# Retention attention followed by a gated two-layer product: the order of the first four pieces' loads and copies, and who copies the last quarter

## The chip, the cores and the metric

The kernel runs on 1 core of one Trainium2 chip. The metric is the time of one execution on the device in microseconds (us). The engines are named as the profile names them: PE (TensorE: matmuls and transposes; PEld is its weight load), ACT (ScalarE), DVE (VectorE), POOL (GpSimd), SP (SyncE, which here only issues DMAs). ACTq and POOLq are the instruction queues of those engines. Each engine takes its instructions in the order written.

## What is computed

The reference, cut to what matters (8 batches, 8 heads, 576 positions, 64 features a head; 4608 tokens, 512 columns, 2048 hidden columns):

```python
scores = (1 / sqrt(D)) * q @ k.transpose(0, 1, 3, 2)
gamma  = 1 - 2 ** (-5 - arange(H))
rel    = pos[:, None] - pos[None, :]
Dmat   = where(rel >= 0, gamma[:, None, None] ** rel, 0)
x      = ((scores * Dmat) @ v)            # then heads side by side: 4608 x 512
h      = x @ w_in                          # 4608 x 2048
g      = h * clip(h + 3, 0, 6) / 6
out    = g @ w_out                         # 4608 x 512, float32
```

## The kernel before

**Pieces.** The sequence of a batch is cut into pieces of 128 positions (four a batch, 32 "main" pieces), and the last 64 positions of two batches make one "rest" piece. The decay is split into a factor on q (`gq`), a factor on v (`gv`, spread out as `gqv[:, 1]`), a 0/1 mask and a state carried from piece to piece. A piece needs: q and k transposed (`qk`, features on partitions), scores `sc` = k q, the masked scores `at` (DVE), v scaled (`vs`, `scale_v`, DVE, in place), the output `o` = `vs` with `at` plus the carried state `tbd` with q, and the new state `u` = k with `vs` plus the old one, scaled by `gfull` into the next `tbd` (DVE). `o` is copied by ACT into `xt`, the input of the first large product.

**The large products.** They go by blocks `kb` of 512 tokens (nine of them). `g1` multiplies `xt` with `win16` (line L577), ACT and DVE make the gate (L585, L586); `g2` (L635), and from the third block `g2_seven` (L720), multiply with `wout16`. Block 0 is made of pieces 0 to 3, so its `g1` can't start before these four are done; later pieces are worked in between units of the large products, in an order written out by hand.

**The first four pieces (`EARLY` = 4)** are worked before any large product. Their k and v come by POOL's queue, which casts them from float32 to float16 on the way (`load_third`, L103; 128 KB written each), in the order k0 v0 k1 v1 k2 v2 k3 v3, then the five parts of `win16`, then the `wout16` parts and later pieces. Their q come plain in float32 by SP's queue into buffers `qf` (`load_q`, L120; 256 KB each), and ACT casts them (`cast_q`, L128). `load_q` can be given an instruction that must be done before the transfer is issued. q is then transposed and scaled in one step by 8 matmuls with `dq`, the diagonal matrices of `gq` (`q_by_pe`); k by 4 transposes (`k_by_pe`); ACT copies each of the two from PSUM into `qk`. In the last of the four, q is copied in two halves, the mask is done in two halves (`scores_last`) and the output too (`out_last`).

`warm` issues matmuls on zeros into a spare PSUM bank. `later` holds DVE operations (mask, state) that `run_later` issues.

Before, the order in the first stretch is:
- q0 and q1 are sent at once; q2 waits for the matmuls of `q_by_pe(0)`, q3 for the transposes of `k_by_pe(0)`.
- DVE: scaling of v0, mask 0, state 0, then per piece c: scaling of v, mask, state.
- ACT: casts, copies, and the two copies that fill `gfull` (L193, L195).

**The end.** In the last block `g2_seven` ends with product x in two PSUM tiles, one for each half u of the last quarter of the output. `copy_half` (L751) copies each on ACT into a buffer `osb`, and `store` (L625) sends it in two halves of 64 rows, one issued by SP and one by ACT. The quarters before go through `total` (L741, DVE) and `store_quarter` (L688): one half from SP, the other from ACT. The `osb` buffers rotate over four.

Of the kernel before, what the change touches and what calls it, by code (L numbers as in the profile page):

```python
# [13 lines left out]
ALU = mybir.AluOpType  # L14
# [3 lines left out]
def kernel(  # L18
# [16 lines left out]
    nc = tc.nc  # L35
    B, H, S, D = q.shape
    NTOK, DM = out.shape
    DFF = moe_w_in.shape[1]
    P = 128
    NPAIR = H // 2  # L40
# [84 lines left out]
                reason="the first pieces have the queues")  # L125

    def cast_q(c):
        nc.scalar.copy(loaded[c]["q16"], plain_q[c])  # L128

    def load_win(f0, f1):  # L130
        return nc.gpsimd.dma_start(
# [11 lines left out]
    nc.gpsimd.iota(wide, pattern=[[1, P + 1]], base=-1, channel_multiplier=-1,  # L143
                   allow_small_or_imprecise_dtypes=True)
    load_q(0)
    load_q(1)
    load_kv(0)
    zeros = const.tile([P, MBLK], FP16)
    nc.vector.memset(zeros, 0.0)
# [6 lines left out]
    for h in range(H):  # L156
# [15 lines left out]
    nc.vector.tensor_tensor(out=ident16, in0=mask01, in1=mask_wide[:, 0:P], op=ALU.subtract)  # L172

    dq = const.tile([P, H, P], FP16)
    nc.vector.tensor_tensor(out=dq, in0=ident16[:, None, :].to_broadcast([P, H, P]),
                            in1=gq[:, :, None].to_broadcast([P, H, P]), op=ALU.mult)
    gqv = const.tile([P, 2, H, D], FP16)
    cast_q(0)
    nc.scalar.copy(gqv[:, 1], gv[:, :, None].to_broadcast([P, H, D]))
# [10 lines left out]
    nc.vector.memset(gfull, 0.0)  # L190

    def fill_gfull():
        nc.scalar.copy(gfull[0:HALF, :, 0:D],  # L193
                       gc[0:HALF, 0, :, None].to_broadcast([HALF, NPAIR, D]))
        nc.scalar.copy(gfull[HALF:P, :, D:2 * D],  # L195
                       gc[HALF:P, 0, :, None].to_broadcast([HALF, NPAIR, D]))

    def fill_gq():
        nc.scalar.copy(gqv[:, 0], gq[:, :, None].to_broadcast([P, H, D]))
# [52 lines left out]
    def k_by_pe(c, tag=None):  # L252
        kn = loaded[c]["kn"]
        pk = bank_or(tag, [P, NPAIR, P], FP16, name=f"trk_{c}")
        for p in range(NPAIR):
            newest[0] = nc.tensor.transpose(pk[:, p, :], kn[:, 2 * p:2 * p + 2, :], ident16)
        nc.scalar.copy(qk_of(c)[:, 1], pk)

    def q_by_pe(c):
        q16, qk = loaded[c]["q16"], qk_of(c)  # L260
        pq = bank([P, NPAIR, P], FP32, name=f"trq_{c}")
        for p in range(NPAIR):
            for h2 in range(2):
                r = slice(h2 * HALF, h2 * HALF + HALF)
                newest[0] = nc.tensor.matmul(
                    pq[r, p, :], q16[:, 2 * p + h2, :], dq[:, 2 * p + h2, :],
                    start=(p == 0), stop=(p == NPAIR - 1), skip_group_check=True)
        if c == EARLY - 1:
            for p in (0, 2):
                nc.scalar.copy(qk[:, 0, p:p + 2], pq[:, p:p + 2])  # L270
        else:
            nc.scalar.copy(qk[:, 0], pq)

    def scores_last(c):

# [60 lines left out]
    def scores(c, late=9):  # L336
        run_later(late)
        qk = st[c]["qk"]
        sc = psum.tile([P, 2, NPAIR, P], FP32, tag="sc", name=f"sc_{c}")
        for p in range(NPAIR):  # L340
            for h2 in range(2):
                r = slice(h2 * HALF, h2 * HALF + HALF)
                nc.tensor.matmul(sc[:, h2, p, :], qk[r, 1, p, :], qk[r, 0, p, :],
                                 start=True, stop=True)
        at = work.tile([P, 2, NPAIR, P], FP16, tag="at", bufs=3, name=f"at_{c}")
        st[c]["at"] = at
        later.append(lambda: nc.vector.tensor_tensor(
            out=at.rearrange("t a b s -> t (a b) s"), in0=sc.rearrange("t a b s -> t (a b) s"),
            in1=mask_b, op=ALU.mult))
# [328 lines left out]
    def store_quarter(kb, i, j, src):  # L678

        cols = slice(NH * j, NH * j + NH)  # L680
        if kb < B:
            r0 = kb * S + TH * i
            nc.sync.dma_start(out[r0:r0 + TH, cols].rearrange("(u p) n -> p u n", u=2), src)
        else:
            rest = out.rearrange("(m x s) n -> x s m n", x=2, s=S)
            for x in range(2):
                queue = nc.scalar if x else nc.sync
                queue.dma_start(rest[x, MAIN:S, 2 * i:2 * i + 2, cols],  # L688
                                src[x * HALF:x * HALF + HALF])

    def g2_seven(kb, last=False):

        gt = gts[kb]

        def w(i, j):
            return wout16[:, KH * i:KH * i + KH, NH * j:NH * j + NH]

        def a(i, j):
            return gt[:, KH * j:KH * j + KH, TH * i:TH * i + TH]

        def s(name):
            return sums[kb, name]

        acc = {}

        def get(name):
            if name not in acc:
                if last and name == "x":
                    acc[name] = [psum.tile([P, NH], FP32, tag=t, name=f"x{t}_{kb}")
                                 for t in ("o", "tu")]  # L710
                else:
                    whole = bank([P, 2, NH], FP32, name=f"{name}_{kb}")
                    acc[name] = [whole[:, 0], whole[:, 1]]
                    wholes[name] = whole
            return acc[name]

        def product(name, u, left, right, first):
            dst = get(name)[u]
            for c in range(KH):
                newest[0] = nc.tensor.matmul(  # L720
                    dst, left()[:, c, P * u:P * u + P], right[:, c, :],
                    start=(first and c == 0 and (u == 0 or name not in wholes)),
                    stop=(c == KH - 1), skip_group_check=True)

        kept, wholes = {}, {}

        def parts(name, tile):
            if name in wholes:
                return [(wholes[name], tile)]
            return [(acc[name][u], tile[:, u]) for u in range(2)]  # L730

        def keep(name):
            kept[name] = work.tile([P, 2, NH], FP32, tag="keep_" + {"m5": "m1"}.get(name, name), bufs=1,
                                   name=f"keep_{name}_{kb}")
            for src, dst in parts({"m5": "z"}.get(name, "x"), kept[name]):
                nc.scalar.copy(dst, src)

        def total(i, j, name, src):
            osb = work.tile([P, 2, NH], FP32, tag="osb", bufs=4, name=f"osb_{kb}_{i}_{j}")
            for (a0, dst), (_, a1) in zip(parts(src, osb), parts(src, kept[name])):  # L740
                nc.vector.tensor_tensor(out=dst, in0=a0, in1=a1, op=ALU.add)  # L741
            store_quarter(kb, i, j, osb)

        def copy_total():
            osb = work.tile([P, 2, NH], FP32, tag="osb", bufs=4, name=f"osb_{kb}_1_0")
            nc.scalar.copy(osb, wholes["x"])
            store_quarter(kb, 1, 0, osb)

        def copy_half(u):
            osb = work.tile([P, NH], FP32, tag="osb", bufs=4, name=f"osh_{kb}_{u}")  # L750
            nc.scalar.copy(osb, acc["x"][u])  # L751
            store(kb, 2 + u, slice(0, NH), osb)

        def unit(name, u, left, right, first, then=()):
            def do():
                product(name, u, left, right, first)
                for f in then:
                    f()
            return do

        plan = [
            ("x", lambda: a(0, 0), w(0, 0), True, [lambda: keep("m1")]),
            ("y", lambda: a(0, 1), w(1, 0), True,
             [lambda: total(0, 0, "m1", "y"), lambda: token_sums(kb, "s3")]),
            ("x", lambda: s("s2"), wts["t2"], False, [lambda: keep("u2")]),
            ("z", lambda: s("s1"), wts["t1"], True,
             [lambda: keep("m5"), lambda: token_sums(kb, "s4")]),
            ("x", lambda: s("s3"), wts["t3"], False, [lambda: total(1, 1, "m5", "x")]),
            ("z", lambda: s("s4"), w(1, 1), False, [lambda: total(0, 1, "u2", "z")]),
            ("x", lambda: a(1, 1), wts["t4"], False, [] if last else [copy_total]),  # L770
        ]
        units = []
        for n, (name, left, right, first, then) in enumerate(plan):
            for u in range(2):
                after = then if u else []
                if last and n == len(plan) - 1:
                    after = [lambda u=u: copy_half(u)]
                units.append(unit(name, u, left, right, first, after))
        return units
# [12 lines left out]
            load(4)  # L792
        load_wout(4 * i, 4 * i + 4)

    scale_v(0)
    q_by_pe(0)
    load_q(2, newest[0])
    warm(2, MBLK)
    cast_q(1)
    k_by_pe(0)  # L800
    load_q(3, newest[0])
    fill_gfull()
    for c in range(EARLY):
        if c:
            inter(c - 1)
# [1 line left out]
        if c < EARLY - 1:  # L807
            scores(c)
            run_later(9)
            if c:  # L810
                k_by_pe(c + 1)
            state_early(c)
            run_later(9)
            if not c:
                k_by_pe(c + 1)
            q_by_pe(c + 1)
            if c + 2 < EARLY:
                cast_q(c + 2)
            scale_v(c + 1)
        else:  # L820
            scores_last(c)
# [280 lines left out]
```

## Time and profile before

| | us |
|---|---|
| median of 3 runs | 294.99 |
| lowest and highest | 293.27, 295.82 |
| the profiled execution's own time | 294.43 |
| its span in the profile | 292.6 |
| PE busy | 281.1 (96%) |
| DVE busy | 227.6 (78%) |
| ACT busy | 169.1 (58%) |
| POOL busy | 104.3 (36%) |
| granted clock of PE | 1.0 |

The profile shows one execution. The page lists busy time by engine, the span in 40 slices, the DMA queues, the chain of work that ended last, and groups of instructions. A row of the timeline gives the start in us, the duration, the engine, the line, the operation, what it writes and reads, and in brackets how long the engine had been idle before and what ended that. For a DMA, "to landing" is the time from the start of its issue to the last of its data.

### The profile page before, as it was taken

The page shows a single profiled execution, that of the slowest core. Times are in us where ns is not written, and L with a number is a line of the kernel's source. Part 1 is how long each engine was busy: PE and PEld are TensorE (multiplying, and loading weights), DVE is VectorE, ACT ScalarE, POOL GpSimd, SP SyncE. Part 2 cuts the span into 40 slices and gives each one's busy share as a digit, 9 for nine tenths or more (in the row PEclk, how much of TensorE's full clock was granted, in tenths as well). Part 3 has the DMA queues.
Part 4 walks back from the last instruction along what each step waited for, and adds up shares of the span by engine and source line. Part 5 has one row for each costly group of instructions (what it writes and reads, how often), then busy time and mean ns, then how long its engine had stood idle before and what let it go on. Part 6 is the DMA issues. An engine that isn't in the chain of part 4 may idle for free.

```text
span 292.6 us, 8351 instructions
## 1 busy us (share of the span) xinstructions
PE 281.1 (96%) x3492; PEld 174.7 (60%) x3492; DVE 227.6 (78%) x377; ACT 169.1 (58%) x301; POOL 104.3 (36%) x130
## 2 busy tenths in 40 slices
PE   7699999999989999999999999999999999999993
PEld 2454445544544587458745874587458745874682
DVE  4858656798758997899789988998899588728860
ACT  6668537784357744774486448644864286338711
POOL 8753578159523432443234324455550000000000
PEclk9999999999999999999999999999999999999999
DMA  9999999999999989997999799979992240120014
GB/s 137 177 205 203 191 157 215 165 126 137 132 215 166 160 85 120 168 141 81 121 163 143 77 127 170 136 82 123 160 139 47 74 110 0 38 81 30 0 39 109
DMA packets 156631, 36.21 MB, mean 124 GB/s; under 512 B 143792, under 2 KB 155568, under 8 KB 156592
## 3 DMA queue, kind: packets, MB, share of 16 engines
q0 software_dynamic: 113104, 17.83, 89.3%
q1 hardware_dynamic: 42896, 17.31, 30.5%
q8 instruction: 27, 0.44, 0.7%
q10 hardware_dynamic: 592, 0.52, 0.5%
q14 instruction: 12, 0.10, 0.1%
HBM read 36.70 MB, written 9.44 MB: 158 GB/s over the span
## 4 chain that ended last, share of the span: by engine, by line
PE 91%; DMA 4%; POOL 2%; DVE 1%; issue 1%; ACT 0%; ACTq 0%; POOLq 0%
PE ph L577 41%; PE x L720 14%; PE pout L635 9%; PE z L720 8%; PE y L720 5%; DMA kn<-in_k_dram 3%; PE o L483 3%; PE sc L450 2%; PE o L504 1%; PE u L535 1%; PE ph L600 1%; POOL kn L103 1%; DMA out_dram<-osb 1%; PE xtu L720 1%; PE xo L720 1%
## 5 line engine op out<-in xcount | busy, mean ns | idle before, releaser
L577 PE MATMUL ph<-xt,win 128*128 128x512 f16 x560 | 122.3, 379 | 0.0
L586 DVE SCALAR_TENSOR_TENSOR gt<-u,ph 128x512 f16<-128x512 f32 x144 | 95.7, 685 | 22.6 <-ACT u L585 21.4
L585 ACT ACTIVATE u<-ph,cb 128x512 f32<-128x512 f32 x144 | 98.4, 688 | 25.7 <-PE ph L577 25.1
L577 PEld LDWEIGHTS <-win 128*128 128x128 f16 x560 | 54.7, 98 | 64.4
L103 POOL DMA_DIRECT2D kn<-in_k_dram x40 | 34.0, 850 | 40.7 <-PE ph L577 15.4
L103 POOL DMA_DIRECT2D qv<-in_v_dram x40 | 33.8, 846 | 38.8 <-PE ph L577 16.2
L720 PEld LDWEIGHTS <-sum_s 128*128 128x128 f16 x448 | 42.7, 98 | 5.3
L103 POOL DMA_DIRECT2D qv<-in_q_dram x36 | 30.2, 839 | 28.7 <-PE z L720 10.4
L720 PEld LDWEIGHTS <-gt 128*128 128x128 f16 x336 | 32.1, 98 | 5.5
L635 PE MATMUL pout<-wout,gt 128*128 128x512 f16 x128 | 29.6, 379 | 0.1
L720 PE MATMUL x<-wsum_t,sum_s 128*128 128x256 f16 x192 | 22.9, 273 | 0.0
L556 ACT CAST tm<-th 128x256 f16<-128x256 f32 x24 | 9.7, 405 | 20.3 <-DVE th L551 20.1
L635 PEld LDWEIGHTS <-gt 128*128 128x128 f16 x128 | 11.9, 98 | 13.2 <-issue 0.4
L456 DVE TENSOR_TENSOR at<-sc,mask 128x1024 f16<-128x1024 f32 x14 | 17.0, 1217 | 1.9 <-PE sc L450 1.9
L676 DVE TENSOR_TENSOR sum_s<-gt 128x1024 f16<-128x1024 f16 (+1 forms) x21 | 18.1, 864 | 0.2
L332 DVE TENSOR_TENSOR qv<-qv,gqv 128x1024 f16<-128x1024 f16 x26 | 17.8, 684 | 0.0
L514 ACT CAST xt<-o 128x512 f16<-128x512 f32 x28 | 15.0, 585 | 4.6 <-PE o L504 4.6
L567 DVE TENSOR_TENSOR ta<-u,th 128x256 f32<-128x256 f32 x24 | 10.2, 424 | 6.3 <-ACT th L554 5.2
L720 PE MATMUL z<-wout,sum_s 128*128 128x256 f16 x112 | 14.5, 274 | 0.0
L720 PE MATMUL y<-wout,gt 128*128 128x256 f16 x112 | 14.3, 273 | 0.0
L720 PE MATMUL z<-wsum_t,sum_s 128*128 128x256 f16 x112 | 13.6, 273 | 0.0
L720 PE MATMUL x<-wout,gt 128*128 128x256 f16 x96 | 11.5, 272 | 0.0
(118 smaller groups left out, 255.3 us busy)
## 6 DMA issues: line engine op xcount, KB each, us to landing
out_dram<-osb SPq DMA_DIRECT2D x32, 256.0 KB, 3.2
kn<-in_k_dram POOLq DMA_DIRECT2D x32, 128.0 KB, 5.9
qv<-in_v_dram POOLq DMA_DIRECT2D x32, 128.0 KB, 6.0
qv<-in_q_dram POOLq DMA_DIRECT2D x28, 128.0 KB, 5.9
wout<-in_moe_w_out_dram POOLq DMA_DIRECT2D x4, 512.0 KB, 15.2
win<-in_moe_w_in_dram POOLq DMA_DIRECT2D x3, 512.0 KB, 12.3
qf<-in_q_dram SPq DMA_DIRECT2D x4, 256.0 KB, 4.6
win<-in_moe_w_in_dram POOLq DMA_DIRECT2D x2, 256.0 KB, 8.3
```

The lines of the kernel that those rows point to most:

```text
L103: loaded[c]["dma"].append(nc.gpsimd.dma_start(dst[p0:p0 + n], src[b, :, s0:s0 + n, :].rearrange("h s d -> s h d")))
L332: scaled = nc.vector.tensor_tensor(out=qv, in0=qv, in1=gqv, op=ALU.mult)
L456: nc.vector.tensor_tensor(out=at.rearrange("t a j p s -> t (a j p) s"), in0=sc.rearrange("t a j p s -> t (a j p) s"), in1=mask64[:, None, ...
L514: nc.scalar.copy(xt_at(cs[0], 0, 2 * P).rearrange("e p (j x s) -> e p j x s", j=2, x=2) [:, :, :, half, :], o[half].rearrange("e j p s -> ...
L556: nc.scalar.copy(tm, ta)
L567: nc.vector.tensor_tensor(out=ta, in0=st[c]["u"][1], in1=st[c]["sum"], op=ALU.add)
L577: newest[0] = nc.tensor.matmul(ph, win16[:, dmc, P * fc:P * fc + P], xt_of(kb)[:, dmc, :], start=(dmc == 0), stop=(dmc == NCC - 1))
L585: nc.scalar.activation(u, ph, ACTF.Relu, bias=cb[:, 0:1], scale=1.0 / 6.0)
L586: nc.vector.scalar_tensor_tensor(out=gts[kb][:, fc, :], in0=u, scalar=1.0, in1=ph, op0=ALU.min, op1=ALU.mult)
L635: nc.tensor.matmul(pout, gt[:, fc, P * mc:P * mc + P], wout16[:, fc, :], start=(fc == 0), stop=(fc == NFC - 1))
L676: nc.vector.tensor_tensor(out=s(which)[:, c0:c1], in0=x(), in1=y(), op=op)
L720: newest[0] = nc.tensor.matmul(dst, left()[:, c, P * u:P * u + P], right[:, c, :], start=(first and c == 0 and (u == 0 or name not in whol ...
```

## The change

- `load_q(1)` is no longer sent at once. q1 waits for the DVE instruction that makes `dq`, and q2 and q3 follow it without a wait of their own.
- ACT's casts of q1 to q3 come later in its order: q(c+1) is cast after the scores of piece c are issued.
- DVE does mask 0 ahead of the scaling of v0 (before: after it).
- The two copies that fill `gfull` go from ACT to DVE, ahead of everything of piece 0.
- The order on PE within the loop changes: piece 0's state comes after the transposes of k1 and q1; in the later pieces the state comes ahead of the next piece's transposes, and in the third turn of the loop q3 is transposed ahead of k3.
- In the last of the four pieces k, not q, is copied in two halves.
- One more `warm` matmul stands between k0's transposes and the scores of piece 0.
- At the end, the second half of the last quarter is copied by DVE instead of ACT, and one half of the quarter with j = 1 in the first row of quarters is stored from POOL instead of ACT.
- `newest` is now set in `scores` instead of `q_by_pe`. Its other uses come after a later matmul that sets it again.

```diff
     load_q(0)
-    load_q(1)
     load_kv(0)
...
-    nc.vector.tensor_tensor(out=dq, in0=ident16[:, None, :].to_broadcast([P, H, P]),
-                            in1=gq[:, :, None].to_broadcast([P, H, P]), op=ALU.mult)
+    load_q(1, nc.vector.tensor_tensor(
+        out=dq, in0=ident16[:, None, :].to_broadcast([P, H, P]),
+        in1=gq[:, :, None].to_broadcast([P, H, P]), op=ALU.mult))
+    for c in range(2, EARLY):
+        load_q(c)
...
     def fill_gfull():
-        nc.scalar.copy(gfull[0:HALF, :, 0:D],
-                       gc[0:HALF, 0, :, None].to_broadcast([HALF, NPAIR, D]))
-        nc.scalar.copy(gfull[HALF:P, :, D:2 * D],
-                       gc[HALF:P, 0, :, None].to_broadcast([HALF, NPAIR, D]))
+        nc.vector.tensor_copy(gfull[0:HALF, :, 0:D],
+                              gc[0:HALF, 0, :, None].to_broadcast([HALF, NPAIR, D]))
+        nc.vector.tensor_copy(gfull[HALF:P, :, D:2 * D],
+                              gc[HALF:P, 0, :, None].to_broadcast([HALF, NPAIR, D]))
...
-        nc.scalar.copy(qk_of(c)[:, 1], pk)                      # k_by_pe
+        if c == EARLY - 1:
+            for p in (0, 2):
+                nc.scalar.copy(qk_of(c)[:, 1, p:p + 2], pk[:, p:p + 2])
+        else:
+            nc.scalar.copy(qk_of(c)[:, 1], pk)
...
-        if c == EARLY - 1:                                      # q_by_pe
-            for p in (0, 2):
-                nc.scalar.copy(qk[:, 0, p:p + 2], pq[:, p:p + 2])
-        else:
-            nc.scalar.copy(qk[:, 0], pq)
+        nc.scalar.copy(qk[:, 0], pq)
...
-                queue = nc.scalar if x else nc.sync             # store_quarter, last block
+                queue = (nc.gpsimd if j > i else nc.scalar) if x else nc.sync
...
-            nc.scalar.copy(osb, acc["x"][u])                    # copy_half
+            if u:
+                nc.vector.tensor_copy(osb, acc["x"][u])
+            else:
+                nc.scalar.copy(osb, acc["x"][u])
...
-    scale_v(0)
+    fill_gfull()
     q_by_pe(0)
-    load_q(2, newest[0])
     warm(2, MBLK)
-    cast_q(1)
     k_by_pe(0)
-    load_q(3, newest[0])
-    fill_gfull()
+    warm(1, MBLK)
     for c in range(EARLY):
         if c:
             inter(c - 1)
             intra(c - 1)
         if c < EARLY - 1:
             scores(c)
             run_later(9)
+            cast_q(c + 1)
             if c:
-                k_by_pe(c + 1)
-            state_early(c)
-            run_later(9)
+                state_early(c)
+                run_later(9)
+            else:
+                scale_v(c)
+            if c == EARLY - 2:
+                q_by_pe(c + 1)
+            k_by_pe(c + 1)
+            if c < EARLY - 2:
+                q_by_pe(c + 1)
             if not c:
-                k_by_pe(c + 1)
-            q_by_pe(c + 1)
-            if c + 2 < EARLY:
-                cast_q(c + 2)
+                state_early(c)
+                run_later(9)
             scale_v(c + 1)
```

More of the change, by code (lines that the diff above doesn't have):

```diff
@@ L127, in cast_q @@
     def cast_q(c):
-        nc.scalar.copy(loaded[c]["q16"], plain_q[c])
+        return nc.scalar.copy(loaded[c]["q16"], plain_q[c])
     def load_win(f0, f1):
@@ L264, in q_by_pe @@
                 r = slice(h2 * HALF, h2 * HALF + HALF)
-                newest[0] = nc.tensor.matmul(
-                    pq[r, p, :], q16[:, 2 * p + h2, :], dq[:, 2 * p + h2, :],
-                    start=(p == 0), stop=(p == NPAIR - 1), skip_group_check=True)
-        if c == EARLY - 1:
-            for p in (0, 2):
-                nc.scalar.copy(qk[:, 0, p:p + 2], pq[:, p:p + 2])
-        else:
-            nc.scalar.copy(qk[:, 0], pq)
+                nc.tensor.matmul(pq[r, p, :], q16[:, 2 * p + h2, :], dq[:, 2 * p + h2, :],
+                                 start=(p == 0), stop=(p == NPAIR - 1), skip_group_check=True)
+        nc.scalar.copy(qk[:, 0], pq)
     def scores_last(c):
@@ L342, in scores @@
                 r = slice(h2 * HALF, h2 * HALF + HALF)
-                nc.tensor.matmul(sc[:, h2, p, :], qk[r, 1, p, :], qk[r, 0, p, :],
-                                 start=True, stop=True)
+                newest[0] = nc.tensor.matmul(sc[:, h2, p, :], qk[r, 1, p, :], qk[r, 0, p, :],
+                                             start=True, stop=True)
         at = work.tile([P, 2, NPAIR, P], FP16, tag="at", bufs=3, name=f"at_{c}")
```

## The prediction

> **What bounds the kernel now.** I read the slices of the page first, to see where TensorE (PE) isn't full.
>
> ```profile
> PE   7699999999989999999999999999999999999993
> PEclk9999999999999999999999999999999999999999
> DMA  9999999999999989997999799979992240120014
> ```
>
> Each digit is a slice of 7.3 us. PE is below 9 in the first two or three slices and in the last; the clock is full throughout. Next the table by windows, for how much that is, and PE's waits after the first main matmul.
>
> ```profile
> 0.00:18.17 18.17, 13.11 (x153) 7.14 (x153) 11.87 (x37) 12.05 (x26) 14.60 (x22) 1.00 1.56 166
> ...
> 120.00:287.80 167.80, 167.71 (x2157) 112.32 (x2154) 137.76 (x213) 95.28 (x165) 40.84 (x52) 1.00 0.90 96
> 287.80:292.60 4.80, 0.00 (x0) 0.00 (x0) 0.00 (x0) 0.40 (x2) 0.00 (x0) 1.00 0.42 111
> ```
>
> ```profile
> PE o L504 <- issue: 0.9, 1, 0.9
> PE o L372 <- DVE qv L245: 0.5, 1, 0.5
> PE o L303 <- DVE at L286: 0.3, 1, 0.3
> ```
>
> The columns after the window are its length and busy PE, weight loads, DVE, ACT, POOL. From 18.17 to 287.8 PE waits 1.7 us in all at most (0.9 of it for nothing that the profile shows, and the 0.3 of L303 falls at 17.9). So the time is A, the start of the first main matmul (L577, 18.17), plus B, a fixed 269.6 of full PE, plus C, the tail of 4.8. The change edits what decides A and C; in B it changes nothing but the start. For A, the chain of waits in the first 25 us:
>
> ```profile
> 6.75 7.55 DMA kn<-in_k_dram
> 14.30 0.05 issue
> 14.34 0.40 PE trk L256 x4
> ...
> 16.20 0.37 PE sc L283 x8
> 16.57 0.02 issue
> 16.59 1.30 DVE at L286 x2
> 17.89 0.04 issue
> 17.93 0.30 PE o L303 x4
> 18.23 6.80 PE ph L577 x31
> ```
>
> The last early K (issued 6.75) lands at 14.30, and A follows 3.87 later. For C, the ACT timeline of the end:
>
> ```profile
> 284.71 2.64 ACTq L688 DMA_DIRECT2D out_dram<-osb  x2
> 287.45 0.37 ACT L751 COPY osh<-xo 128x256 f32<-128x256 f32 x1 [4.30 <-DMA out_dram<-osb]
> 287.86 0.51 ACTq L625 DMA_DIRECT2D out_dram<-osh  x1
> 288.49 0.37 ACT L751 COPY osh<-xtu 128x256 f32<-128x256 f32 x1 [0.66 <-ACT osh L751]
> 288.89 0.51 ACTq L625 DMA_DIRECT2D out_dram<-osh  x1
> ```
>
> PE's last two groups (xo, xtu) end at 286.84 and 287.71. The copy of xo starts only at 287.45: the wait is put down to a DMA, but the store that used that buffer belongs to the block before. What stands ahead of it in ACT's queue is the issue of a store (286.7, 0.63 us). Copy, issue, copy, issue then run in series on ACT, and the last store is issued at 288.89, 1.2 after PE is done.
>
> **The tail (C), step by step.** That half store moves to POOL, so ACT is free when xo ends: copy 286.9 to 287.27, issue at 287.3. The second copy goes to DVE, idle since 286.7: from 287.76, 0.42 us (DVE's add of the same 128x256 shape, L741, took 0.42; a copy reads one operand less), so done at 288.18, and SP and ACT issue the last stores at 288.2 instead of 288.89. SP has two issues of 0.5 to 0.6 from 286.7 on and is free at 287.9. The last store then lands 2.0 to 2.2 later as before (L625), and the end follows. Gain: 0.65 us. The POOL store's cost isn't in the trace, POOL having written nothing to memory; nearest are its 64-row loads (L103 after 200 us): issue 0.68, landing 2.8 to 5.3 after the start of the issue, median 3.9, against 2.5 to 2.9 for the ACT store. From 286.7 that is 289.5 to 292.0; the last store lands at 290.3. I take 3.9 (290.6, a cost of about 0.2 against the gain in the worst reading) as hidden, since the 5.3 belongs to the time when loads queued; the bounds are 0 and 1.7. Nothing is queued behind it on POOL.
> The Trainium skill, "DMA: Bandwidth & Descriptors", Latency and other measured facts, speaks against moving a store there: first byte at about 1 us from GpSimd, 0.6 from SP and ACT. By that page the store would land 0.4 later than ACT's 2.9, near 290.0, still covered; no row here shows a POOL store.
>
> **The front (A): when data lands.** Landing is the issue plus the time to landing of single issues. Before: Q0 3.96, Q1 5.26, K0 6.12, V0 7.01, K1 7.91, V1 8.69, Q2 10.49, K2 11.04, V2 12.85, Q3 13.37, K3 14.30, V3 15.08, first weights 16.15. These follow the order in which the issues end, whichever queue they are on (V1 5.05, Q2 5.70, K2 5.93, V2 6.80, Q3 6.96, K3 7.68). So it is one line of transfers, always full, and moving the Qs reorders it without shortening it.
> After: SP's Q1 waits for the dq operation of DVE (2.37 plus 1.23, 3.60). Queued behind it on SP are Q2 and Q3, and then only the output store of 42.11. The three issues end near 4.1, 4.5 and 4.9; POOL's K0, V0, K1, V1 at 2.4, 3.3, 4.2, 5.05. Order: Q0 K0 V0 Q1 K1 Q2 Q3 V1 K2 V2 K3 V3.
> Prices: a K or V 0.88 (V0 to K1 0.90, K1 to V1 0.78). A Q: 0.99 (256 KB at the 265 GB/s of the window 3 to 4 us) to 1.47 (V1 to K2 is 2.35, less 0.88); Q0 to Q1 is 1.30, with the start-up in it. I take 1.2. K0 without Q1 ahead: 1.36 plus the 3.4 to 3.7 of an unhindered load, and 0.15 for its longer issue, 5.2.
> Sums: V0 6.1, Q1 7.3, K1 8.2, Q2 9.4, Q3 10.6, V1 11.4, K2 12.3, V2 13.2, K3 14.1, V3 15.0. K0 is 0.9 sooner, which buys nothing: the two warm matmuls hold PE to 6.1. K3 is 0.2 sooner, but K2 is 1.3 later and V1 2.7 later.
>
> **The front: what follows from it.** Durations are the rows of before (casts and copies on ACT 0.59 to 0.62, the next one 0.49 after; mask 1.23; state scaling 0.69; V scaling 0.42; transposes 0.40).
> Piece 0: transposes 6.1, its scores 7.2, as now; the extra warm matmul (about 0.45) lies in the 0.7 that PE waits for ACT's copy. The two fills, now on DVE, cost 0.40 each on ACT; on DVE they run from 5.4 to about 6.2, where DVE idles to 7.11; cover gone, they would delay the first mask by 0.8. First mask ahead of first scaling saves nothing, since V0 lands before the scores exist.
> Piece 1: K1 8.2, copies of K and Q to 9.7, scores 9.8 (before 9.52). Then DVE has V1's scaling ahead of mask 1, and V1 lands at 11.4: mask 1 runs 11.85 to 13.1 (before 9.95). This is the new wait; behind it on DVE stand the state of piece 1, V2's scaling and mask 2.
> Piece 2: K2 12.3, transposes to 12.75, copies of K and Q to 13.9, scores 13.95, mask 2 14.4 to 15.6.
> Piece 3: PE's queue has scores 2, state 2, Q3, K3. Q3's cast stands behind the output copy of piece 1 on ACT (13.9 and 14.4 to 15.0), so Q3 goes at 15.05 and K3's transposes at 15.3, though K3 has been there since 14.1. Copy of Q3 15.45, K3 in halves from 15.95, scores 16.3 (before 16.13), masks 16.65 to 17.95, outputs, A at 18.4. K in halves shortens K3 to A from 3.87 to 3.1, but K3 no longer decides: K2 plus 6.1 does.
> The first weights land 1.07 after V3, at 16.1; they don't bind. The second quarter landed at 20.43 before and is used at 21.6, so A may move by 0.3 freely.
>
> **The sum.** Front +0.25 (18.4 less 18.17), tail -0.65: -0.4. The profiled execution took 294.43 (span 292.6 and 1.8 around it); it gives 294.0. It lay 0.19% under the median of 294.99, and the runs span 293.27 to 295.82, so the range needs about a microsecond each way for that alone.
>
> **Rivals.** (1) Slower: all three Qs go ahead of K1 on the engines. For it: from 8.0 to 8.5 us, with Q2 in flight, the DMA engines moved almost only Q2's rows (197 GB/s against 143 to 148 with K and V alone). Against: Q3, issued at 6.59, let V2 pass. Then K1 lands at 10.6, its chain (K1 plus 8.6, a mask, a state scaling and a V scaling per piece on DVE) puts A at 19.2: +1.05 - 0.65 = +0.4, 294.8; with a Q at 1.47 K1 is at 11.4, A at 20.0, 295.6. It decides from K1 landing after 10.2. (2) The Qs cost 0.99 and don't hold up K2: K2 11.7, A 17.8, or, if K2 stays at 11.0, K3 13.8 plus 3.3 is 17.1; total -1.0 to -1.7, 292.7 to 293.4. For it: fewer switches between queues; against: the mixed rows above. (3) POOL's store lands last, 5.3 after its issue, at 292.0: the end is 0.9 later than before instead of 0.65 sooner, 295.6. That the Qs are not sent together can't be: behind Q1's wait SP has nothing else to wait for.
> The Trainium skill, "DMA: Bandwidth & Descriptors", Queues, rings and completion order, has each DMA engine take packets from its queues in turn, not by arrival. By that rule V1 goes ahead of Q3 and lands near 10.3, mask 1 runs earlier, and A is 18.3, 0.1 under my sum. The trace's V2 ahead of Q3 speaks for arrival.
>
> **How the numbers follow.** Forecast 0.52 (its own range 293.0 to 295.2), rival 1 0.22, rival 2 0.18, rival 3 0.08. All lie within 1.5 us of before, and 1% (2.95 us) is about what a measurement of this kernel can tell from no change. Faster by over 1% needs the best of rival 2 and a low run, 0.07; slower by over 1% rivals 1 and 3 together or a high run, 0.08; within 1% 0.85. Range: rival 2 less half a microsecond of spread, 292.3, to rivals 1 and 3 with a little, 296.0.
>
> **What would show it.** Right: Qs landing ahead of V1 and K2; DVE's wait before mask 1 or the scaling ahead of it put down to V1; PE no longer waiting for K3; the first main matmul at 17.8 to 18.8; ACT's copy of xo at 286.9 plus the shift of A, DVE's copy beside it, and the last issue 0.5 after PE's end instead of 1.2. Wrong: K1 after 10.2, K2 before 11.5, a POOL store landing after the last ACT store, or a B other than 269.6.

## The result and the profile after

| | before | after |
|---|---|---|
| median (18 runs each, same chip) | 293.86 | 295.98 |
| lowest and highest | 293.05, 295.82 | 294.42, 297.77 |
| the profiled execution (span) | 294.43 (292.6) | 295.67 (293.9) |

The changed kernel is slower: ratio 1.0064, interval 1.0043 to 1.0085. The forecast was 0.4 us faster. After's page starts like this:

```profile
PE   7699999999999999999999999999999999999993
PEclk9799999999999999999999999999999999999999
```

The slices of PE look almost as before; only the second digit of the clock row is lower. The table by windows, cut at the start of the first main matmul (19.70) and near the end of PE's work, shows what moved (columns as in the prediction).

```profile
0.00:19.70 19.70, 15.19 (x154) 8.04 (x154) 12.56 (x39) 11.20 (x24) 14.57 (x22) 0.91 1.46 157
19.70:289.41 269.71, 268.04 (x3343) 167.50 (x3340) 215.72 (x340) 156.52 (x274) 90.10 (x109) 1.00 1.18 121
289.41:293.90 4.49, 0.00 (x0) 0.00 (x0) 0.42 (x1) 0.00 (x0) 0.00 (x0) 0.98 0.43 119
```

In before PE's last matmul ended at 287.71, so its three parts are 18.17, 269.54 and 4.94. After has A +1.53, B +0.17, C -0.45: together +1.25, and the two profiled executions differ by 1.24. The loss is in the front. PE's waits say where it begins:

```profile
PE trk L258 <- DMA kn<-in_k_dram: 2.2, 1, 2.2
...
```

This wait is new: PE stands 2.2 us for K1. In before K1's transposes had no wait on their row:

```profile
7.96 0.40 PE L256 MATMUL trk<-ident,kn 128*128 128x128 f16 x4
```

Before's waits for K2 (1.17) and K3 (1.00) are gone, since PE now comes to them later. The timeline of after's front, PE and DVE:

```profile
7.14 0.40 PE L344 MATMUL sc<-qk 64*128 64x128 f16 x8 [0.25 <-ACT qk L263]
9.71 0.40 PE L258 MATMUL trk<-ident,kn 128*128 128x128 f16 x4 [2.17 <-DMA kn<-in_k_dram]
...
11.48 0.61 PE L344 MATMUL sc<-qk 64*128 64x128 f16 x8
...
13.32 0.61 PE L258 MATMUL trk<-ident,kn 128*128 128x128 f16 x4
...
16.49 0.40 PE L258 MATMUL trk<-ident,kn 128*128 128x128 f16 x4
```

```profile
11.77 0.43 DVE L247 TENSOR_TENSOR qv<-qv,gqv 128x512 f16<-128x512 f16 x1
12.13 1.22 DVE L348 TENSOR_TENSOR at<-sc,mask_wide 128x1024 f16<-128x1024 f32 x1
```

K1's transposes start at 9.71 (9.67 is its landing), V1 is scaled the moment it lands (11.74), mask 1 follows at 12.13, K2's transposes start at 13.32 (landing 13.27). K3's start at 16.49 without a wait in brackets, a microsecond after K3 landed (15.46). From 10.4 to 13.8 PE's groups take 0.59 to 0.64 instead of 0.40, which is the lower clock.

Landings, last of the 16 engines:

| | K0 | V0 | Q1 | K1 | Q2 | V1 | K2 | V2 | Q3 | K3 | V3 |
|---|---|---|---|---|---|---|---|---|---|---|---|
| before | 6.12 | 7.01 | 5.26 | 7.91 | 10.49 | 8.69 | 11.04 | 12.85 | 13.37 | 14.30 | 15.08 |
| forecast | 5.2 | 6.1 | 7.3 | 8.2 | 9.4 | 11.4 | 12.3 | 13.2 | 10.6 | 14.1 | 15.0 |
| after | 4.87 | 7.83 | 9.11 | 9.67 | 10.84 | 11.74 | 13.27 | 14.62 | 14.79 | 15.46 | 16.35 |

From V0 on everything is later than forecast, and the line ends 1.3 later than before. The DMA engines' rate shows where the line falls behind. Window 3 to 4 us of before, then of after; the last column is GB/s:

```profile
3.00:4.00 1.00, 1.00 (x4) 0.18 (x2) 0.82 (x6) 0.01 (x1) 1.00 (x2) 1.00 1.29 265
```

```profile
3.00:4.00 1.00, 1.00 (x4) 0.17 (x2) 0.83 (x6) 0.23 (x1) 1.00 (x2) 1.00 1.47 105
```

Q0's packets end at 3.1 in before and 3.3 in after. In before Q1's follow at once (middle packet, the start of the median one of its 1024, 3.55) and then K0's (4.51), V0's (5.41), K1's (6.32). In after nothing follows but K0 (3.84) and V0 (5.20), whose POOL issues end at 2.40 and 3.29; Q1, issued at 3.6, comes at 6.41 and K1 at 7.38. Through V0 after has moved one Q (256 KB) less and is only 0.2 sooner.

The tail of after:

```profile
288.57 0.37 ACT L755 COPY osh<-xo 128x256 f32<-128x256 f32 x1 [3.73 <-PE xo L721]
288.69 0.62 POOL L689 DMA_DIRECT2D out_dram<-osb  x1 [69.11 <-DVE osb L742]
288.97 1.43 ACTq L626 DMA_DIRECT2D out_dram<-osh  x2
289.10 1.42 SPq L626 DMA_DIRECT2D out_dram<-osh  x2
289.44 0.42 DVE L753 COPY osh<-xtu 128x256 f32<-128x256 f32 x1 [1.06 <-PE xtu L721]
```

ACT's copy now waits for PE's xo and nothing else, DVE copies xtu right after PE's end (289.41), and the last stores are issued at 289.9, 0.5 after it (before: 1.2).

### The profile page after: what moved, and what is told of

Read it like the earlier page. It is cut to its first block, busy times and chain, and to the rows that moved or that the text cites. A ratio compares the mean times of both kernels' runs of the same rounds, so it can differ in the third digit from the quotient of the medians.

```text
span 293.9 us, 8353 instructions
## 1 busy us (share of the span) xinstructions
PE 283.2 (96%) x3493; PEld 175.5 (60%) x3493; DVE 228.7 (78%) x380; ACT 167.7 (57%) x298; POOL 104.7 (36%) x131
## 4 chain that ended last, share of the span: by engine, by line
PE 92%; DMA 3%; DVE 1%; issue 1%; POOL 1%; ACT 1%; POOLq 0%
PE ph L578 41%; PE x L721 14%; PE pout L636 9%; PE z L721 9%; PE y L721 5%; DMA qv<-in_v_dram 3%; PE o L484 3%; PE sc L451 2%; PE o L505 1%; PE u L536 1%; PE ph L601 1%; PE xtu L721 1%; PE xo L721 1%; PE trk L258 1%; POOL kn L103 1%
## 5 line engine op out<-in xcount | busy, mean ns | idle before, releaser
L721 PEld LDWEIGHTS <-sum_s 128*128 128x128 f16 x448 | 42.7, 98 | 5.3
L103 POOL DMA_DIRECT2D qv<-in_q_dram x36 | 30.2, 839 | 30.9 <-PE z L721 10.4
L721 PEld LDWEIGHTS <-gt 128*128 128x128 f16 x336 | 32.1, 98 | 5.5
L689 POOL DMA_DIRECT2D out_dram<-osb x1 | 0.6, 617 | 69.1 <-DVE osb L742 69.1
L721 PE MATMUL x<-wsum_t,sum_s 128*128 128x256 f16 x192 | 22.9, 273 | 0.0
L568 DVE TENSOR_TENSOR ta<-u,th 128x256 f32<-128x256 f32 x24 | 10.2, 424 | 6.8 <-ACT th L555 5.8
L721 PE MATMUL z<-wout,sum_s 128*128 128x256 f16 x112 | 14.5, 274 | 0.0
L721 PE MATMUL y<-wout,gt 128*128 128x256 f16 x112 | 14.3, 273 | 0.0
L721 PE MATMUL z<-wsum_t,sum_s 128*128 128x256 f16 x112 | 13.6, 273 | 0.0
```

What stands on the lines that cost most here:

```text
L103: loaded[c]["dma"].append(nc.gpsimd.dma_start(dst[p0:p0 + n], src[b, :, s0:s0 + n, :].rearrange("h s d -> s h d")))
L568: nc.vector.tensor_tensor(out=ta, in0=st[c]["u"][1], in1=st[c]["sum"], op=ALU.add)
L721: newest[0] = nc.tensor.matmul(dst, left()[:, c, P * u:P * u + P], right[:, c, :], start=(first and c == 0 and (u == 0 or name not in whol ...
```

## The experiments

Two theories of the loss were tried first: that the late Qs make K1 late, and that the front runs at half the clock because PE stands still. "Rate" is the mean over 3 to 4 us, A the start of the first main matmul; ratios are to the kernel before on the same chip. Rate, landings and A are of one profiled execution of each kernel. The low rate of after from 3 to 4 us is called the hole.

| kernel | ratio (95%) | rate | K1 | K2 | V3 | A |
|---|---|---|---|---|---|---|
| before | 1 | 265 | 7.91 | 11.04 | 15.08 | 18.17 |
| after | 1.0064 (1.0043, 1.0085) | 105 | 9.67 | 13.27 | 16.35 | 19.70 |
| 1: Q as before | 0.9969 (0.9943, 0.9995) | 270 | 8.07 | 11.04 | 14.81 | 18.61 |
| 2: Q1 at once | 1.0039 (1.0014, 1.0065) | 275 | 9.99 | 12.68 | 15.26 | 20.57 |
| 3: warm in the gap | 1.0063 (1.0039, 1.0088) | 91 | 10.00 | 13.14 | 16.86 | 19.78 |
| 4: tail only | 0.9989 (0.9962, 1.0017) | 262 | 8.04 | 11.87 | 15.72 | 19.92 |
| 5: more warm | 0.9996 (0.9968, 1.0024) | 279 | 8.05 | 11.12 | 15.08 | 17.82 |
| 6: all Q at once | 1.0079 (1.0050, 1.0107) | 268 | 10.69 | 12.49 | 15.10 | 21.46 |
| 7: last piece as before | 0.9980 (0.9954, 1.0006) | 267 | 8.10 | 11.11 | 14.92 | 18.56 |
| 8: Q1 alone late | 1.0046 (1.0020, 1.0071) | 84 | 9.93 | 13.86 | 17.28 | 21.41 |
| 9: Q1 at 2.1 us | one run | 76 | 9.13 | 12.19 | 15.92 | 19.39 |
| 10: Q1 at 5.1 us | one run | 102 | 7.57 | 12.16 | 16.91 | 21.27 |

A also carries the clock of its execution. PE's groups were at half the clock (0.61 instead of 0.40) for about 3.4 us of the front in after and experiments 1, 9 and 10, for 6.8 in 2 and 8, and until 13.4, 16.3 and 17.2 in 7, 4 and 6. In before, 3 and 5 they were at 0.40 from 7.7 us on at the latest.

**1. Everything of the change but the late Qs.**

```diff
-    load_q(1, <the DVE operation that makes dq>); load_q(2); load_q(3)
+    load_q(1)                       # at once, behind load_q(0)
...
     q_by_pe(0)
+    load_q(2, newest[0])
...
     k_by_pe(0)
+    load_q(3, newest[0])
```

> The changed kernel with the four Q transfers sent as before (Q1 at once, Q2 after the matmuls of q_by_pe(0), Q3 after the transposes of k_by_pe(0)); all else as changed. Theory 1 (the sends): landings return to those of before (K1 7.9, K2 11.0, K3 14.3), PE's wait of 2.2 us for K1 goes, the granted clock stays 1.0 and the first main matmul starts near 17.5, 0.7 before that of the kernel before (K in halves and Q3 ahead of K3 then pay); with 0.45 from the tail the time is 1.1 us under before, ratio 0.996. Rival (the new order on PE, ACT and DVE costs the time): the start stays above 19, ratio above 1.004.

K1 and K2 land as before the change, and this kernel's ratio to before is below 1 with its whole interval (median 294.0 of 12 runs, before 294.87 of 35). PE, in the front:

```profile
8.11 0.40 PE L256 MATMUL trk<-ident,kn 128*128 128x128 f16 x4 [0.25 <-DMA kn<-in_k_dram]
```

The wait for K1 is 0.25 instead of 2.17. The late Qs alone cost what the change loses, and more: from 0.9969 to 1.0064 is 0.95%, some 2.8 us, and the two intervals don't overlap. Of all kernels run this is the one to keep, the only one whose interval lies below 1.

The start near 17.5 did not come. This execution began its main matmuls at 18.61, 0.44 later than before's, with PE's groups at half the clock from 9.8 to 13.4; its span is still 0.3 shorter, by a tail of 4.45. What the kernel gains over before beyond its tail is not shown by the profiles.

**2. Q1 at once, Q2 and Q3 behind `dq`.**

```diff
+    load_q(1)
-    load_q(1, <dq>); load_q(2); load_q(3)
+    load_q(2, <dq>); load_q(3)
```

> The changed kernel with Q1 sent at once behind Q0, Q2 and Q3 still behind dq. If one late transfer (Q1, and K1 behind it) makes the loss: K0 lands near 6.1, K1 near 8, PE's longest wait falls under 1.3, start 17.7 to 18.2, ratio 0.997 to 1.000. If two queues in use at the same time cost the engines their rate, whichever Q it is: K2 still lands after 12.3 and K3 after 14.8, start 18.4 to 19, ratio 1.000 to 1.004.

The line is whole again (275 GB/s, V3 15.26), but Q2 now goes ahead of K1 and Q3 ahead of V1:

```profile
10.04 0.61 PE L259 MATMUL trk<-ident,kn 128*128 128x128 f16 x4 [2.35 <-DMA kn<-in_k_dram]
```

PE waits as long for K1 as in after, and the kernel is slower than before. So a Q ahead of K1 does harm without the hole. What the hole adds in time is not shown by this pair: after's ratio is higher, but the intervals overlap.

**8. Only Q1 late.**

```diff
     load_q(1, <dq>)
-    load_q(2); load_q(3)
+    load_q(2, newest[0])            # behind q_by_pe(0), as before
+    load_q(3, newest[0])            # behind k_by_pe(0), as before
```

> The changed kernel with only Q1 behind dq; Q2 waits for the matmuls of q_by_pe(0), Q3 for the transposes of K0, as before. Theory 1, in the form that Q1 taking its turn ahead of K1 is enough: K1 lands 1 us or more later than in run 1 (8.1), at 9 to 9.5, start at 18.5 or later at the full clock, ratio 1.000 to 1.004. In the form that only three Qs in a row do harm (run 2 had two and K1 at 10.0): K1 at 8.1 to 8.8, start within 0.4 of run 1, ratio 0.996 to 0.999.

One late Q is enough for both: the hole (84 GB/s), K1 at 9.93 with a wait of 3.2 us, V3 at 17.28, and a ratio above 1 with its whole interval.

**6. All four Qs at once at the start.**

```diff
-    load_q(0)
+    for c in range(EARLY):
+        load_q(c)
```

> Run 1's kernel with all four Q sent at once at the start, with no wait. By arrival (the prediction's rule) Q1, Q2 and Q3 land at about 5.3, 6.3 and 7.3 and K0 only near 8.2, K1 near 10; start near 19. By turns between the two queues (the page's rule) K0 lands at 6 to 6.8 with Q2 and Q3 behind it, and from then on Q and K or V alternate: K1 9.5 or later. Either way K1 is late, and theory 1 expects a start of 18.5 to 19.5 and a ratio of 1.001 to 1.006; if only the wait for dq were harmful, the start is 17.5 to 18 and the ratio 0.997.

No hole (268 GB/s) and a line no longer than before (V3 15.10), yet the highest ratio of all (from 6 runs; its interval overlaps after's): Q1, K0, Q2, V0, Q3, K1 arrive in this order and K1 lands at 10.69. The run was meant to tell whether transfers go by the order in which their issues end, or whether the engines take SP's and POOL's queues in turn. It can't: SP's issues took up to 0.96 us here and ended at 1.84, 2.80 and 3.80, POOL's at 2.41, 3.30 and 4.17, so both rules give this order.

**3. Eight matmuls on zeros in PE's wait for K1.**

```diff
             cast_q(c + 1)
+            if not c:
+                warm(8, MBLK)
```

> The changed kernel with 8 more warm matmuls (zeros into a spare bank) on PE behind the scores of piece 0, in the 2.2 us that PE waits for K1. Theory 2 (the halved clock from 10.4 to 13.5 us makes the loss): granted clock 1.0 from 7 us on, matmul groups back to 0.4 us, the start falls from 19.7 by 1 us or more, ratio near 1.000. Theory 1 (the landings make it): landings unchanged (K2 13.3, K3 15.5), the start falls by 0.4 at most, to 19.3, ratio 1.003 or more.

The clock stays full, and the start hardly differs from after's (19.78 against 19.70):

```profile
10.05 0.40 PE L258 MATMUL trk<-ident,kn 128*128 128x128 f16 x4 [0.61 <-DMA kn<-in_k_dram]
```

The ratio is after's (1.0063). The clock falls as the main cause: with 0.40 throughout, K1 at 10.00 and K2 at 13.14 give the late start by themselves. (The profiled execution also lost 2 us behind the start, `x` L721 waiting 1.6 for nothing that the profile shows; the others of this kernel were not traced.)

**5. Experiment 1 with more matmuls on zeros, to keep the clock full.**

```diff
-    warm(7, MBLK)
+    warm(8, MBLK)
...
     k_by_pe(0)
-    warm(1, MBLK)
+    warm(2, MBLK)
...                                  # and 2 behind scores 0, 3 ahead of state 0
```

> Run 1's kernel (the changed one with the Q transfers sent as before) with more matmuls on zeros in PE's early waits: 8 instead of 7 at the start, 2 instead of 1 behind K0's transposes, 2 behind the scores of piece 0, 3 ahead of the state of piece 0. Run 1 started its first main matmul at 18.6, and the chain worked with its own landings at the full clock gives 17.5; its groups took 0.6 instead of 0.4 us from 10 to 13.3. Theory 2 in its smaller form (the halved clock costs 0.4 to 1.8 us of the start, in executions where it falls into the front): granted clock 1.0 from 7 us on, start 17.4 to 17.8, mean clock of the runs above run 1's 0.997, ratio 0.994 or so against 0.997. Rival (the chain lacks something else): clock full, start still above 18.2.

In the profile the start is the earliest of all (17.82, span 291.8), 0.8 before experiment 1's with landings no earlier. The runs don't show it: 0.9996, an interval that holds both 1 and experiment 1's ratio. What the half clock costs over many executions stays open.

**4. The two edits of the tail alone.**

```diff
-                queue = nc.scalar if x else nc.sync
+                queue = (nc.gpsimd if j > i else nc.scalar) if x else nc.sync
...
-            nc.scalar.copy(osb, acc["x"][u])
+            if u:
+                nc.vector.tensor_copy(osb, acc["x"][u])
+            else:
+                nc.scalar.copy(osb, acc["x"][u])
```

> The kernel before with only the two edits of the end (second half of the last quarter copied by DVE, one half store from POOL). From the last matmul's end to the end of the span: 4.94 before, 4.49 in the changed kernel. If the tail gains what it showed there: 0.45 us, ratio 0.9985, the start at 18.2 as before. If the POOL store landed last or delayed the others: no gain, ratio 1.000 to 1.003.

From PE's end (289.53) to the end of the span (294.0) is 4.47, as in after and 0.47 less than before: the gain is there in the profile, and too small for the interval. With the front of before, this execution started its main matmuls at 19.92, not 18.17, and its PE groups say why:

```profile
8.18 0.61 PE L314 MATMUL u<-qv,kn 128*128 128x128 f16 x4
...
15.52 0.61 PE L256 MATMUL trk<-ident,kn 128*128 128x128 f16 x4
```

It ran at half the clock until 16.3, where the profiled execution of before had 0.40 from 6.2 on. The loads explain 0.6 to 0.8 of the 1.75 (K3 landed 0.60 and K2 0.83 later than in before); the rest goes with the half clock.

**7. Experiment 1 with the last piece as before** (K whole, Q in halves, K3's transposes ahead of Q3's).

```diff
-            if c == EARLY - 2:
-                q_by_pe(c + 1)
             k_by_pe(c + 1)
-            if c < EARLY - 2:
-                q_by_pe(c + 1)
+            q_by_pe(c + 1)
```

> Run 1's kernel with the last of the four pieces worked as before: K3 transposed ahead of Q3, K copied whole, Q in halves. If the halves of K pay what the prediction said (K3 to the first main matmul 3.1 instead of 3.87), this run has 3.6 or more, a start 0.3 to 0.8 later at the same clock, ratio 0.998 to 1.000. If they don't decide, ratio as run 1's, 0.997.

A is 18.56 against 18.61, the ratios overlap. From K3's transposes to A it is 3.52 against 3.21, so the halves gain 0.3 there; but in experiment 1 these transposes stand behind Q3's (15.40, with K3 there since 14.08), and at A nothing of the gain is seen. The clocks of the two executions were not alike, so this settles only that K in halves doesn't decide.

**9 and 10. The hole by itself: Q1 released sooner and later** than `dq`, Q2 and Q3 as before.

```diff
-    load_q(1, <dq, done at 3.60>)
+    load_q(1, <ident16, done at 2.03>)          # 9
+    load_q(1, newest[0])  # behind q_by_pe(0)   # 10
```

> Edit: as the run in which only Q1 is held back, but Q1 waits for the DVE operation that makes ident16 (1.80 to 2.03 in the traces) instead of dq (2.37 to 3.60); Q2 and Q3 as before the change. In all three kernels with Q1 behind dq the 16 DMA engines end a K or V 2.2 to 4.4 us apart from V0 on (0.4 to 1.9 in the others), and the stretch from 3 to 6 us moves 102 to 119 GB/s against 188 to 199. Theory G (a gap: K0 and V0 alone don't fill the engines from 3 to 6 us, and a Q whose issue comes only at 3.6 can't fill it): issued at 2.1, Q1 is there in time, 3 to 6 us moves 175 GB/s or more, Q1 lands by 6.0, K1 by 8.6, V3 by 15.7, the engines end within 1.9 us, A 17.5 to 19 depending on the clock. Theory O (Q1 behind POOL's first K on the engines puts them out of step, whenever it is issued): spread 2.2 us or more, V3 after 16.2, K1 after 9.3, A after 19.5.

> Edit: as the run in which only Q1 is held back, but Q1 waits for the matmuls of piece 0's q (end at 5.1 in the traces) instead of dq (3.60), with Q2 behind it in the same queue; Q3 as before the change. Theory G: the stretch from 3 to 6 us moves 120 GB/s or less, one Q less than before, and the whole line is a Q longer: V3 16.1 or later on all engines, its first share too (13.8 to 14.3 in all kernels so far) after 15. Theory O (out of step because Q1 comes in while K0 and V0 start up, 3.6 to 5.5 us): issued at 5.1 it comes into a running stream, as Q2 did before the change, the engines end within 1.9 us, and V3 lands by 15.7. Both: Q1 lands 8.5 or later, K1 after 9, PE waits over 2 us for K1 or Q1, A after 19.5.

Window 3 to 4 us of experiment 9:

```profile
3.00:4.00 1.00, 1.00 (x4) 0.17 (x2) 0.82 (x6) 0.10 (x1) 1.00 (x2) 1.00 0.71 76
```

Neither theory fits whole. Released at 2.1 us Q1 is already too late for the hole (76 GB/s; theory G had it in time), though it takes its place in the order ahead of V0. V3 lands 0.84 later than in before while the engines end mostly within 1.5 us of each other, so the hole may lengthen the line alone; but this is one execution, and experiment 4 had V3 at 15.72 without a hole.

Released at 5.1 the hole is the same (102), and no Q goes ahead of K1. Both theories had K1 after 9; it landed at 7.57, 0.34 sooner than in before, and the long wait is for Q1 (landed 10.43) and its cast on ACT:

```profile
7.61 0.40 PE L255 MATMUL trk<-ident,kn 128*128 128x128 f16 x4 [0.66 <-DMA kn<-in_k_dram]
11.12 0.41 PE L268 MATMUL trq<-dq,qv 128*64 128x128 f16 x8 [3.11 <-ACT qv L128]
```

So the hole by itself doesn't make K1 late; a Q ahead of K1 does. The engines, within 1.1 us up to K1, come apart to 2 or 3 us from V1 on, where Q1's rows come in. (The 2.2 to 4.4 us of the other three kernels are 2.0 to 4.4 in the traces.) That speaks against theory O's "start-up" as the place, and theory G's later first share of V3 (over 15) didn't come either (13.86). The single runs took 294.55 (experiment 9) and 296.67 (experiment 10), and 294.12 for before beside them.

Taken together: all five kernels that hold Q1 back have the hole (76 to 105 GB/s) and V3 at 15.9 to 17.3; all seven that send it at once have 262 to 279 and V3 at 14.8 to 15.7. In four of the five the fastest engine ends V3 at 13.8 to 14.3, as in before (13.96), and the slowest 2.2 to 3.5 later (before 1.1): part of the longer line is engines out of step, and a transfer has landed only with the slowest. What puts them out of step isn't settled.

## Why the prediction was wrong, by its own steps

**The line of transfers: the step that failed.** "One line of transfers, always full, and moving the Qs reorders it without shortening it" was used as if it couldn't lengthen either. The line of before was full from 3 to 4 us because Q1 stood directly behind Q0. Without it, in after, the engines moved 105 GB/s from 3 to 4 us and 83 from 4 to 5, with K0 and V0 and the end of Q0. The forecast gave K0 its gain (5.2, measured 4.87), and then put V0 one price of 0.88 behind it, at 6.1. That price was read where K and V alone moved at 143 to 148 GB/s; why they are slower at the start isn't settled. V0's middle packet came 1.36 behind K0's, and its slowest engine landed at 7.83. K1 was forecast 0.3 later than before (8.2) and landed 1.76 later (9.67): 1.06 of it by the middle packet (6.32 to 7.38), the rest by the engines' spread.

Experiment 10 splits the two terms, as far as one execution can. With K0, V0 and K1 in a row and no Q between them, the forecast's own prices put K1 at 7.0; it landed at 7.57, so holding Q1 back bought 0.34 against before instead of 0.9. Q1's place ahead of K1 was priced at 1.2; from 7.57 to 9.67 it is 2.1, of which 1.3 by the middle packet (6.09 to 7.38) and the rest because the engines came apart (K1's last 1.1 behind its first there, 2.3 in after).

**The issues.** SP's were to end near 4.1, 4.5 and 4.9. They ended at 4.00, 4.63 and 7.01: the third took 2.34 us instead of the 0.4 that these ends imply. So Q3 went behind V2, and only Q2 stood between K1 and V1. With the measured ends, the order of the issues' ends is exactly the order of after's packets, so that part of the reading held, and the same is so in all twelve traces. The rule that was cited has engines taking their queues in turn (the Trainium skill, "DMA: Bandwidth & Descriptors", Queues, rings and completion order). In after that is no test: Q and K or V alternate under both rules. Before speaks against turns by whole transfers: V2's middle packet (10.31) came ahead of Q3's (11.31), though Q3's issue had ended at 6.96 and K2's packets at 9.80.

**What follows from the landings.** The chain was right in its parts. Mask 1 stands behind V1's scaling (forecast 11.85, measured 12.13); K3 no longer decides; A follows K2 by 6.43 (forecast 6.1). K2 was 0.97 later than forecast (13.27 for 12.3), and with the 0.33 of the longer chain behind it, part of which ran at half the clock, that is the whole difference between A at 18.4 and 19.70.

**The clock.** "The clock is full throughout" was read from one execution and taken for the kernel's. Experiment 4 has the same front and started 1.75 later, at half clock until 16.3. Over the runs, a mean granted clock of 0.996 or more was found in 24 of before's 63 runs beside the experiments, in 9 of 12 of experiment 1, but in none of after's 18 and none of experiment 8's 9. That would fit a low clock that goes with PE's wait for K1. But experiment 6, with a wait of 1.7, has 3 of 6, and the mean can miss the front: experiment 4's profiled execution has 0.999. So the link stays open. The profiled pair differs by 1.24 us, the runs by 0.64%, 1.9 us; the other 0.65 may be the clock, but experiment 3, at a mean of 0.994, was no faster, so it is not shown.

**The rivals.** Rival 1 had the mechanism (a Q ahead of K1, PE waiting, the chain of piece 1 late) and the size (294.8 to 295.6; the profiled execution was 295.67, the median 295.98), but a wrong way there: all three Qs ahead of K1, and a threshold of 10.2. One Q was enough, at 9.67 (experiment 8: 9.93). It had been given 0.22, because the trace's V2 ahead of Q3 was taken as evidence against it; but there Q3's issue had ended after V2's (6.96, 6.80), and in the changed kernel Q1's ends ahead of K1's (4.00, 4.17). Rival 3 didn't happen: POOL's store, issued at 288.69, landed at 291.43, 2.7 later, before the last store (292.32). The Trainium skill, "DMA: Bandwidth & Descriptors", Latency and other measured facts, has the first byte at about 1 us from POOL against 0.6 from ACT. The later landing that was estimated from it didn't come: ACT's stores of the same 128 KB took 3.0 and 3.1.

**The tail.** The copies and issues went as forecast; the gain was 0.45 to 0.47 instead of 0.65, because the store that lands last now took 2.4 from its issue (SP's; 2.0 before), where before it was ACT's with 2.2.

**Hidden parts.** The two fills ran on DVE from 5.14 to 6.03, and DVE then waited 1.55 for the scores, so they cost nothing. Mask 0 ahead of the scaling of V0 came to cover V0's lateness (mask 7.58 to 8.80, V0 at 7.83), which was not foreseen, as V0 was to come at 6.1.

## What to carry to other kernels

Before a transfer is held back, look at the half microseconds after it in the DMA rate: if it is what fills the engines until the next queue's data comes, holding it back gains little for what is behind it (K1 0.34 us in experiment 10), and its full price is paid later in the line. Count the order of arrival by when each issue ends, with the durations of issues that come back to back on one queue, and follow the first transfer that the busiest engine waits for (here K1), not the last. Look at several executions before a clock is called full: the durations of equal groups show it.

## What the runs showed of the hardware that was not expected

- Half the clock comes and goes from execution to execution in a front of short matmuls: the same groups took 0.40 in before and 0.61 in experiment 4. The stretches were about 3.4 us long or a multiple (10.39 to 13.8 in after, 9.83 to 13.4 in experiment 1, 11.4 to 18.2 in experiment 8), also where PE had stood still for no more than 0.7 (experiment 1). The Trainium skill, "TensorE: Matmul & The Clock Gate", Part 1: The HAM clock gate, puts the clock at 4/8 after an idle window of about 3.4 us, and calls its phase variable from run to run. The length and the variation agree with these rows. A fully idle window isn't in them (the longest stand of PE in any of these fronts is 3.2), so stretches began here without one.
- The clock column can miss it: it reads 1.00 from 10 to 16 us of experiment 6, whose groups there take 0.61 to 0.64.
- The third of three back-to-back issues on SP took 2.34 us (2.27 in experiment 3, 2.51 in experiment 10). Single ones took 0.37 to 0.56, but Q3's in experiment 8 took 1.46.
- The two fills of the same 64x256 shape took 0.22 and 0.65 on DVE; why the second is longer was not tried.
